# Filter rows moved behind a read-back, a stage placed three steps later, the last block split over four banks, and one product placed earlier

## The chip, the cores and the metric

The kernel runs on one core of one Trainium2 chip. The metric is the device time of one execution in microseconds (us). It is quoted as the median of several runs, with their range. The span of the profiled execution, which the profile measures, is some 2 to 3 us shorter than that time.

PE is TensorE's matmul, DVE is VectorE, ACT is ScalarE, POOL is GpSimd and SP is SyncE, which here only issues DMAs. An engine's name with a q behind it (SPq) is its sequencer, where DMA issues are recorded.

## The reference

```python
def _attn_ref(x, filt_r, filt_i):           # x: 8 x 3008 x 256
    X = np.fft.rfft(x, axis=1)
    F = (filt_r + 1j * filt_i)[None, :, :]
    return np.fft.irfft(X * F, n=x.shape[1], axis=1)

def _moe_ref(x, w_in, w_out, beta):         # 24064 tokens, 256 -> 2048 -> 256
    h = x @ w_in
    g = h * (1.0 / (1.0 + np.exp(-beta * h)))
    return g @ w_out
```

Each batch is filtered along its 3008 positions in the frequency domain. The result goes token by token through a feed-forward layer with a gated sigmoid.

## The kernel before

The feed-forward layer is the bulk: 47 blocks of 512 tokens, each in 16 steps, so 752 steps. A step has two large matmuls into `hps`, one ACT activation into `gT`, and four matmuls into `acc`. PE needs about 0.87 us for it, which is the distance from one activation to the next.

The filter is made of matmul stages. Batch 0 is filtered before the first step (the start). Batches 1 to 7 are filtered in pieces that a plan puts between the steps. For each of them the stages are: `s1` (first transform, written to a DRAM scratch d1), `a2_read` (d1 read back in another order), `s23` (second transform, spectrum times filter, first inverse transform), then a second trip through DRAM (d2), and `s4`. The "spectrum" below is `s23`; its first matmul needs the landed d1 read.

```python
# issue of the filter's rows, at the end of the start
for i in range(4):
    scale_wout(i)            # w_out was staged in frr's rows; POOL scales it out of there
for k0 in range(0, NK, JG):  # k0 = 0: SP issues; k0 = 8, 16, ...: POOL
    for at in (0, M):
        for go in load_filter(frr, filt_r, at, k0, JG, gp if k0 else nc.sync):
            go()             # 12 loads in all, 256 KB each
# ... cut ...
def s1(b, i, on_act):        # cut to the write
    ...
    if jj + 2 == JG:
        nc.sync.dma_start(s["d1r"][:, g * JG : (g + 1) * JG, :], s["a1"][:])

def a2_read(b):              # four reads, which wait until the writes have landed
    for h in range(NG):
        t = a2pool.tile([P, KG, D], BF16, name="a2", tag="a2")
        nc.sync.dma_start(t[:], s["d1c"][:, h * KG : (h + 1) * KG, :])
# ... cut ...
if B > 1:                    # batch 1's plan: place(first step, last step, pieces)
    at = place(1, 11, u1(1, True), per=2)
    place(at + 1, at + 1, [lambda: a2_read(1)], per=9)
    at = place(22, 54, u23(1), per=2)
    place(58, 58, [lambda: zz_read(1)], per=9)
    place(66, 78, u4(1), per=2)
# ... cut: the last block ...
acc = [opsum.tile([P, 2, D], F32, name="acc", tag="acc") for _ in range((nch + 1) // 2)]
...
    evac(ost[:, 2 * h : 2 * h + n, :], acc[h][:, :n, :], h == 0 and (i < 6 or last))
    if last:
        store(t0 + 2 * h * P, n * P, ost[:, 2 * h :, :], (nc.scalar, nc.sync)[h])
```

In the start, batch 0's first stage and the angle tables come interleaved:

```python
    for i in range(3, 5):
        first1(i, (False, False))
        warm(2)                      # matmuls on zeros, to keep PE occupied
    t2_more(0, nc.vector)            # three DVE copies within SBUF (lines 289 to 291)
    first1(5, (True, True))
```

## Time and profile before

| | before |
|---|---|
| median of 3 runs (range) | 794.76 us (793.23 to 795.56) |
| span of the profiled run | 791.4 us |
| start, up to batch 0's first `zz` transposes | 35.99 us |
| steps 0 to 100 (with the filter of batches 1 and 2) | 112.33 us |
| steps 100 to 751 | 633.40 us |
| tail, from the start of the last activation to the end | 6.03 us |

The four pieces, with 3.61 us between the transposes and step 0, make up the span. They are read from the start times of the 752 activations in the trace.

The page of the kernel before, cut to the busy times and the chain of work that ended last:

```profile
span 791.4 us, 15358 instructions
PE 776.2 (98%) x6097; PEld 547.4 (69%) x6097; DVE 393.2 (50%) x641; ACT 597.9 (76%) x920; POOL 149.3 (19%) x151
...
PE 88%; DMA 6%; DVE 3%; issue 1%; ACT 1%; SPq 0%; POOL 0%; DVEq 0%; POOLq 0%; ACTq 0%
```

Only 15 us of the span remain in which PE is not busy, and part of these is at the two ends. But 6% of the chain is DMA, so there are places where PE waits for a transfer. PE's waits, longest sum first (waiting tile and line, what it waited for: us in total, how many, the longest):

```profile
PE ps L621 <- DMA a<-d: 2.3, 2, 2.1
PE psa L347 <- DMA xg<-in_x_dram: 1.2, 1, 1.2
```

The first is the spectrum's first product in batches 1 and 2, waiting for the d1 read. The transfers behind the longer one are on SP's timeline (start, duration, sequencer, line, output from input, how many issues):

```profile
54.73 0.30 SPq L604 DMA_DIRECT2D d<-a  x1
62.77 1.78 SPq L611 DMA_DIRECT2D a<-d  x4
64.60 2.62 SPq L760 DMA_DIRECT2D out_dram<-ost  x4
```

and the product on PE's timeline, with its wait in brackets:

```profile
66.34 0.38 PE L621 MATMUL ps<-a,t 128*128 128x256 bf16 x2 [2.10 <-DMA a<-d]
```

The last d1 write is issued at 54.73 and the reads, which wait for its landing, go at 62.77. That is 8.0 us for a write of 384 KB. What else the DMA engines did is in the window view (busy time of each engine in the window; the last three columns are PE's granted clock, the DMA engines' busy share and what they moved in GB/s):

```profile
41.00:59.00 18.00, 17.91 (x143) 12.26 (x142) 7.19 (x11) 15.07 (x27) 8.21 (x10) 1.00 1.05 259
59.00:67.00 8.00, 5.90 (x51) 4.16 (x50) 2.08 (x4) 4.78 (x8) 0.00 (x0) 1.00 0.67 203
```

From 41 to 59 us the engines are full. POOL has issued eight filter loads of 256 KB there, among the d1 writes. The first and the last of the eight on POOL's timeline:

```profile
47.85 0.58 POOL L129 DMA_DIRECT2D frr<-in_filt_r_dram  x1
...
51.73 0.60 POOL L132 DMA_DIRECT2D frr<-in_filt_r_dram  x1
```

### The profile page before, as it was taken

The page shows a single profiled execution, that of the slowest core. Times are in us where ns is not written, and L with a number is a line of the kernel's source. Part 1 is how long each engine was busy: PE and PEld are TensorE (multiplying, and loading weights), DVE is VectorE, ACT ScalarE, POOL GpSimd, SP SyncE. Part 2 cuts the span into 40 slices and gives each one's busy share as a digit, 9 for nine tenths or more (in the row PEclk, how much of TensorE's full clock was granted, in tenths as well). Part 3 has the DMA queues.
Part 4 walks back from the last instruction along what each step waited for, and adds up shares of the span by engine and source line. Part 5 has one row for each costly group of instructions (what it writes and reads, how often), then busy time and mean ns, then how long its engine had stood idle before and what let it go on. Part 6 is the DMA issues. An engine that isn't in the chain of part 4 may idle for free.

```text
span 791.4 us, 15358 instructions
## 1 busy us (share of the span) xinstructions
PE 776.2 (98%) x6097; PEld 547.4 (69%) x6097; DVE 393.2 (50%) x641; ACT 597.9 (76%) x920; POOL 149.3 (19%) x151
## 2 busy tenths in 40 slices
PE   8898999999999999999999999999999999999997
PEld 5766667766777667876668766687667776776665
DVE  7846835755537464465534746267452761500000
ACT  6886886886678866788677876778767788677776
POOL 8542500330013200131002310024000340000000
PEclk9999999999999999999999999999999999999999
DMA  9994678116811178011960228412360214110101
GB/s 189 243 258 134 165 193 219 55 67 186 208 52 47 68 200 218 29 68 71 216 179 28 90 95 196 152 42 90 120 203 27 75 67 127 43 39 28 54 27 53
DMA packets 82579, 91.43 MB, mean 116 GB/s; under 512 B 3726, under 2 KB 72480, under 8 KB 81486
## 3 DMA queue, kind: packets, MB, share of 16 engines
q1 hardware_dynamic: 78460, 71.06, 28.9%
q0 software_dynamic: 3328, 18.35, 11.7%
q10 hardware_dynamic: 720, 1.05, 0.5%
q8 instruction: 47, 0.77, 0.4%
q14 instruction: 24, 0.20, 0.1%
HBM read 57.16 MB, written 46.66 MB: 131 GB/s over the span
## 4 chain that ended last, share of the span: by engine, by line
PE 88%; DMA 6%; DVE 3%; issue 1%; ACT 1%; SPq 0%; POOL 0%; DVEq 0%; POOLq 0%; ACTq 0%
PE acc L811 39%; PE hps L783 38%; PE ps L599 3%; DMA d<-a 2%; PE ps L522 2%; PE ps L621 2%; PE ps L647 2%; DMA fri<-in_filt_i_dram 1%; DVE ost L107 1%; DMA a<-d 1%; DMA xg<-in_x_dram 1%; DVE q_t L636 0%; ACT a L105 0%; DVE q_t L633 0%; DVE p_t L632 0%
## 5 line engine op out<-in xcount | busy, mean ns | idle before, releaser
L792 ACT ACTIVATE gT<-hps,beta_sb 128x512 bf16<-128x512 f32 x752 | 516.7, 687 | 177.6 <-PE hps L783 167.3
L811 PE MATMUL acc<-wout_sb,gT 128*128 128x256 bf16 x3008 | 454.9, 272 | 1.1 <-ACT ost L105 0.2
L783 PE MATMUL hps<-y,win_sb 128*128 128x512 bf16 (+7 forms) x1728 | 447.7, 351 | 0.3 <-DVE y L109 0.3
L811 PEld LDWEIGHTS <-gT 128*128 128x128 bf16 x3008 | 285.4, 98 | 132.3 <-issue 4.2
L783 PEld LDWEIGHTS <-win_sb 128*128 128x128 bf16 x1728 | 164.8, 98 | 24.8 <-issue 0.7
L637 POOL TENSOR_TENSOR v_t<-p_t,q_t 128x512 bf16<-128x512 f32 x84 | 106.8, 1271 | 370.2 <-DVE q_t L636 363.5
L107 DVE COPY ost<-acc 128x512 f32<-128x512 f32 x87 | 56.1, 683 | 195.3 <-PE acc L811 189.1
L107 DVE CAST a<-ps 96x512 bf16<-96x512 f32 x96 | 65.9, 686 | 86.6 <-PE ps L599 86.6
L109 DVE TENSOR_SCALAR y<-ps 128x376 bf16<-128x376 f32 (+2 forms) x120 | 64.5, 541 | 61.2 <-PE ps L522 61.0
L632 DVE TENSOR_TENSOR p_t<-ps,frr 128x512 f32<-128x512 f32 x84 | 58.1, 692 | 34.4 <-PE ps L621 29.3
L636 DVE TENSOR_TENSOR q_t<-ps,fri 64x512 f32<-64x512 f32 x84 | 58.3, 694 | 1.2
L633 DVE SCALAR_TENSOR_TENSOR q_t<-ps,fri 64x512 f32<-64x512 f32 x84 | 57.4, 684 | 1.1
L522 PEld LDWEIGHTS <-zz 96*128 96x128 bf16 x512 | 35.3, 97 | 29.6 <-DVE q_t L636 0.8
L105 ACT ACTIVATE z<-ps 128x512 bf16<-128x512 f32 x84 | 49.5, 590 | 0.4
L599 PE MATMUL ps<-xg,t 94*96 94x512 bf16 x112 | 41.9, 381 | 0.1
L522 PE MATMUL ps<-t,zz 96*128 96x94 bf16 x448 | 36.7, 204 | 0.0
L621 PE MATMUL ps<-a,t 128*128 128x256 bf16 x168 | 32.1, 273 | 2.3 <-DMA a<-d 2.3
L116 POOL DMA_DIRECT2D xg<-in_x_dram x22 | 12.3, 566 | 116.4 <-PE acc L811 97.7
L647 PE MATMUL ps<-v_t,t 128*128 128x256 bf16 x168 | 32.1, 273 | 0.3 <-DVE q_t L636 0.3
L621 PEld LDWEIGHTS <-t 128*128 128x128 bf16 x168 | 15.9, 98 | 17.1 <-issue 2.7
L599 PEld LDWEIGHTS <-t 94*96 94x96 bf16 x112 | 13.8, 123 | 11.9
L647 PEld LDWEIGHTS <-t 128*128 128x128 bf16 x168 | 15.4, 98 | 8.0 <-DVE q_t L636 0.5
(121 smaller groups left out, 198.7 us busy)
## 6 DMA issues: line engine op xcount, KB each, us to landing
out_dram<-ost SPq DMA_DIRECT2D x40, 512.0 KB, 2.8
d<-a SPq DMA_DIRECT2D x28, 384.0 KB, 6.4
a<-d SPq DMA_DIRECT2D x28, 384.0 KB, 4.8
d<-z SPq DMA_DIRECT2D x28, 384.0 KB, 2.6
zz<-d SPq DMA_DIRECT2D x28, 384.0 KB, 5.6
xg<-in_x_dram POOLq DMA_DIRECT2D x6, 1280.0 KB, 10.5
out_dram<-ost SPq DMA_DIRECT2D x20, 128.0 KB, 2.4
frr<-in_moe_w_out_dram POOLq DMA_DIRECT2D x4, 512.0 KB, 14.7
```

What stands on the lines that cost most here:

```text
L107: nc.vector.tensor_copy(dst, src)
L109: nc.vector.tensor_scalar_mul(dst, src, scale)
L522: nc.tensor.matmul(ps[:, e, :NP], lhsT=zz[:, jj + e, dc * P : (dc + 1) * P], rhs=tab[:], start=True, stop=True,)
L599: nc.tensor.matmul(ps[:KP], lhsT=t1[:], rhs=s["x"][:, 2 * i : 2 * i + 2, :], start=True, stop=True)
L621: nc.tensor.matmul(ps[:, e, :], lhsT=t2[:, k0 + e, 3:5, :].rearrange("p c k -> p (c k)"), rhs=s["a2"][g][:, kk + e, :], start=True, stop=True,
L632: nc.vector.tensor_tensor(p_t[:], ps[:], frr[:, ks_, :], ALU.mult)
L636: nc.vector.tensor_tensor(q_t[:M], ps[M:P], fri[M:P, ks_, :], ALU.mult)
L637: nc.gpsimd.tensor_tensor(v_t[:], p_t[:], q_t[:], ALU.add)
L647: nc.tensor.matmul(ps[:, e, :], lhsT=t3[:, k0 + e, :], rhs=v_t[:, e, :], start=True, stop=True)
L783: nc.tensor.matmul(hps[:, pos - t0 : pos - t0 + ln], lhsT=win_sb[:, dc, fb * P : (fb + 1) * P], rhs=ys[b][:, dc, n0 : n0 + ln], start=(dc ...
L792: nc.scalar.activation(gT[:, :tn], hps[:, :tn], ACT.Silu, scale=beta_sb[:, fb : fb + 1])
L811: nc.tensor.matmul(acc[tb // 2][:, tb % 2, :], lhsT=gT[:, tb * P : (tb + 1) * P], rhs=wout_sb[:, fb, :], start=(fb == 0 and tb % 2 == 0), ...
```

## The change

The intent: take the eight filter loads out of the d1 writes' way by queueing them on SP behind the d1 reads (rows 8 and up are needed only at the fifth spectrum product); give batch 1's spectrum three more steps; evict the last block in four halves with four stores; and move the first product of the start, and one eviction, where DVE should take them better. The diff, cut to its core:

```diff
@@ the start: first product moved up, one eviction from ACT to DVE
-    table3(0, 2, True)
-    table3(0, 0, False)
 ...
+    table3(0, 2, True)
+    product(0)
+    table3(0, 0, False)
     for i in range(NK // 2 + FLAG):
-        if i < NK // 2:
+        if 0 < i < NK // 2:
             product(i)
 ...
-            table3(1 + i // 3, 4 - 2 * (i % 3), i % 3 == 1 or i == 8)
+            table3(1 + i // 3, 4 - 2 * (i % 3), i % 3 == 1)
@@ the filter's rows
-    for k0 in range(0, NK, JG):
-        for at in (0, M):
-            for go in load_filter(frr, filt_r, at, k0, JG, gp if k0 else nc.sync):
-                go()
+    for at in (0, M):
+        for go in load_filter(frr, filt_r, at, 0, JG, nc.sync):
+            go()
 ...
+    def uf():                       # rows 8 and up
+        return [
+            go
+            for k0 in range(JG, NK, JG)
+            for at in (0, M)
+            for go in load_filter(frr, filt_r, at, k0, JG, nc.sync)
+        ]
@@ batch 1's plan
-        place(at + 1, at + 1, [lambda: a2_read(1)], per=9)
-        at = place(22, 54, u23(1), per=2)
-        place(58, 58, [lambda: zz_read(1)], per=9)
-        place(66, 78, u4(1), per=2)
+        place(at + 1, at + 1, [lambda: a2_read(1)] + uf(), per=9)
+        at = place(25, 56, u23(1), per=2)
+        place(60, 60, [lambda: zz_read(1)], per=9)
+        place(67, 79, u4(1), per=2)
@@ the last block: one bank, one eviction and one store for each 128 rows
+                    (fpsum if h % 2 else opsum).tile([P, 1, D], F32, name="acc", ...)
 ...
-                        store(t0 + 2 * h * P, n * P, ost[:, 2 * h :, :], (nc.scalar, nc.sync)[h])
+                        store(t0 + h * P, P, ost[:, h:, :], (nc.sync, nc.scalar)[h // 2])
```

## The prediction

> **What bounds it.** The page's busy line gives PE 776.2 of 791.4 us (98%) at full clock; the chain that ended last is 88% PE, 77 points of it the two large products (acc, hps). The Trainium skill ("Perfetto Trace Analysis", Identifying the Most-Contended Engine) warns that PE busy is no measure of the limit; here it only tells where PE idles. The change leaves the matrix work as it is, so it can win only idle time. PE's waits sum to about 9 us. The largest: 2.3 us in two waits of batch 1's and 2's first spectrum product (ps, L621) on the d1 read-back, the longer 2.1 us at 64.2 to 66.3. The rest are pieces of 0.2 to 1.2 us.
>
> **1. Filter rows behind the d1 reads.** In the window view the DMA engines are saturated (share 0.9 to 1.2) from 41 to 59 us. There POOL issues 8 frr loads of 256 KB (47.8 to 51.7) among the d1 writes. The last d1 write is issued at 54.7, lands 7.9 us later, and only at 62.8 can the reads go (3.5 us). "DMA: Bandwidth & Descriptors" (Issuing engines are not separate DMA queues) says that transfers of different issuers share the same 16 engines and interleave; the saturated share agrees. Without these loads I expect (estimate from about 230 GB/s here) the write to land at 57 to 60, the first read at 61 to 64.
>
> **2. Spectrum three steps later.** Step 25 begins near 67 us (three steps of 0.87 plus the work placed in them). Either move alone should remove the 2.1 us wait. The burst behind it (PE waiting 0.31 on DVE q_t at 74) should go too. Gain 2.1 to 2.5 us. Filter rows 8 and up are first needed at the fifth product, near 76 us; I expect them by 70 to 74.
>
> **3. Given back.** Batch 1's d2 read moves about 2 us later, into a stretch where DMA is saturated again (110 to 130). There batch 2's last d1 write takes 11.5 us, and its read reaches PE with no slack (0.17 us wait at 134.7). I expect that wait to become 0 to 2 us, about 0.7.
>
> **4. Start.** From 21.9 to 34.9 us DVE runs almost without gaps: it waited 0.86 us for fri rows, then works through products of 2 x 0.60. Moving the first product up 0.3 us only lengthens that wait. One t3b eviction goes from ACT (0.83) to DVE (a slot of 0.46), where it just fills the 0.46 us gap at 32. Net 0, within 0.3.
>
> **5. End.** Evictions of 0.60 (ACT) and 0.69 (DVE) and two stores of 256 KB become four half evictions (0.35 to 0.42, an estimate) and four stores of 128 KB (2.4 against 2.8 us to land). The last issue is no earlier, since two stores of 0.4 queue on each engine. Net -0.1, within 0.3.
>
> **Sum.** -2.3 + 0.7 + 0 - 0.1, and up to 0.4 more: about -2 us. 794.76 becomes **792.7 us**, 8 in 10 within **790.8 to 794.5**. Faster by over 2%: 0.01; within 2%: 0.98; slower: 0.01. Before's own runs spread by 2.3 us, so the sign is likely, not sure.
>
> **Signs.** Right if PE's L621 wait at 64 is gone, the last d1 write lands in under 5 us, no DVE p_t waits on frr, and the span is about 789.5. Step 3 shows in the L621 wait near 133. Step 4: zz's first transposes stay near 36.0.
>
> **Wrong if** the frr rows[...] come later than 76 us; if block 0's stores behind them hold the output tile; if the second d1 wait grows by more than 2 us; or if the start becomes DVE-bound.

## The result, and the profile after

| | before | after |
|---|---|---|
| median of 6 runs (range) | 794.45 us (793.23 to 795.56) | 791.66 us (789.83 to 793.29) |
| ratio, with its 95% interval | | 0.9965 (0.9944 to 0.9986) |
| span of the profiled run | 791.4 us | 790.8 us |
| start | 35.99 us | 38.38 us |
| steps 0 to 100 | 112.33 us | 110.18 us |
| steps 100 to 751 | 633.40 us | 633.42 us |
| tail | 6.03 us | 5.18 us |

A ratio here and below is the mean time of one kernel's runs over the mean of the other's runs of the same rounds, so it is not quite the ratio of the medians. The changed kernel is faster by 0.35%, which counts as the same within 2%. All outputs are right.

The table holds a puzzle. The middle won 2.15 us and the tail 0.85 us, but the profiled run's start was 2.39 us longer, so the span won only 0.6 us. The six times explain which is typical: 789.83, 789.99, 790.43 and 792.89, 793.05, 793.29. They are two groups, and the profiled run belongs to the slower one. The experiments have to say whether the start is a cost of the change.

The same lines of the page after:

```profile
span 790.8 us, 15274 instructions
PE 772.1 (98%) x6001; PEld 548.0 (69%) x6097; DVE 395.7 (50%) x643; ACT 596.9 (75%) x920; POOL 144.6 (18%) x143
...
PE 92%; DVE 3%; issue 2%; POOL 2%; ACT 1%; DVEq 0%; ACTq 0%; POOLq 0%
```

DMA has left the chain. The fall of PE's busy time from 776.2 to 772.1 is not saved work: weight loads still number 6097, while matmul records fell to 6001, because some are missing from this trace. PE's longest waits after:

```profile
PE psa L347 <- DMA xg<-in_x_dram: 2.8, 2, 2.3
PE pw L186 <- DVE wz L181: 1.2, 1, 1.2
PE pb L409 <- POOL tiny L308: 0.9, 1, 0.9
```

No wait on L621 is left, in batch 1 or 2. What leads now is the start: the waits for rows of x grew from 1.2 us (one) to 2.8 us (two, the longer one 2.28), and a wait of 0.9 us is new. The view puts that one down to POOL's `tiny`; but the product that waits, at 17.09 us, reads `a_t`, whose eviction DVE ended at 16.99. SP's timeline after:

```profile
57.11 0.30 SPq L604 DMA_DIRECT2D d<-a  x1
60.31 1.77 SPq L611 DMA_DIRECT2D a<-d  x4
62.18 0.37 SPq L129 DMA_DIRECT2D frr<-in_filt_r_dram  x1
```

The last d1 write now lands 3.2 us after its issue, not 8.0, and the filter loads follow the reads. The product starts without a bracket:

```profile
69.23 0.38 PE L621 MATMUL ps<-a,t 128*128 128x256 bf16 x2
```

The same windows as before:

```profile
41.00:59.00 18.00, 17.46 (x130) 11.59 (x131) 8.82 (x14) 15.35 (x29) 5.00 (x3) 1.00 0.70 185
59.00:67.00 8.00, 7.95 (x69) 5.80 (x68) 2.52 (x4) 6.18 (x11) 0.00 (x0) 1.00 0.79 251
```

The DMA share from 41 to 59 us fell from 1.05 to 0.70. PE is busy for 7.95 of the 8 us from 59 to 67, where it had 5.90. DVE's `p_t` products, which read the rows that come later now, show no wait for them.

**Batch 2's read.** The prediction feared a longer wait there. Before, from the chain that ended last (start, duration, what):

```profile
118.05 0.56 DVE y L109
118.61 0.12 SPq L760
...
119.89 11.48 DMA d<-a
...
131.38 3.28 DMA a<-d
...
134.71 0.38 PE ps L621 x2
```

After, SP's timeline and PE's:

```profile
119.86 0.57 SPq L604 DMA_DIRECT2D d<-a  x1
131.30 1.77 SPq L611 DMA_DIRECT2D a<-d  x4
```

```profile
134.94 0.38 PE L621 MATMUL ps<-a,t 128*128 128x256 bf16 x2
```

The write takes as long as before (11.4 us from its issue to the reads). But the steps are 0.6 us later on the clock in this run (step 80 starts at 132.21, before at 131.63) and the read is not, so it has slack and the wait of 0.17 us is gone.

**The tail.** Before, the last activation (ACT's timeline) and the last store (SP's):

```profile
785.33 0.69 ACT L792 ACTIVATE gT<-hps,beta_sb 128x512 bf16<-128x512 f32 x1 [0.18 <-PE hps L783]
...
787.44 0.37 SPq L746 DMA_DIRECT2D out_dram<-ost  x1
```

After (the last two stores are ACT's):

```profile
785.58 0.69 ACT L800 ACTIVATE gT<-hps,beta_sb 128x512 bf16<-128x512 f32 x1 [0.18 <-PE hps L791]
...
787.33 0.88 ACTq L754 DMA_DIRECT2D out_dram<-ost  x2
```

The last issue is not earlier: before it begins 2.11 us after the activation's start, after it begins about 2.19 us after it (half of the 0.88 for the first of two). The trace's packets show what is: the last store packet ends 4.35 us after the activation before, and 3.85 us after it in the changed kernel.

### The profile page after: what moved, and what is told of

It reads as the page before. It is cut to its first block, busy times and chain, and to the rows that moved or that the text cites. A ratio compares the mean times of both kernels' runs of the same rounds, so it can differ in the third digit from the quotient of the medians.

```text
span 790.8 us, 15274 instructions
## 1 busy us (share of the span) xinstructions
PE 772.1 (98%) x6001; PEld 548.0 (69%) x6097; DVE 395.7 (50%) x643; ACT 596.9 (75%) x920; POOL 144.6 (18%) x143
## 3 DMA queue, kind: packets, MB, share of 16 engines
q10 hardware_dynamic: 736, 1.05, 0.6%
## 4 chain that ended last, share of the span: by engine, by line
PE 92%; DVE 3%; issue 2%; POOL 2%; ACT 1%; DVEq 0%; ACTq 0%; POOLq 0%
PE acc L826 42%; PE hps L791 37%; PE ps L599 3%; PE ps L522 3%; PE ps L621 2%; PE ps L647 2%; DVE ost L107 1%; POOL xg L116 0%; POOL r L269 0%; DVE qb_t L442 0%; ACT a L105 0%; DVE pb_t L442 0%; PE pb L409 0%; PE psz L452 0%; DVE q_t L636 0%
## 5 line engine op out<-in xcount | busy, mean ns | idle before, releaser
L791 PE MATMUL hps<-y,win_sb 128*128 128x512 bf16 (+7 forms) x1634 | 427.4, 350 | 0.3 <-DVE y L109 0.3
L107 DVE COPY ost<-acc 128x512 f32<-128x512 f32 (+1 forms) x88 | 56.2, 677 | 193.6 <-PE acc L826 188.0
L522 PEld LDWEIGHTS <-zz 96*128 96x128 bf16 x512 | 35.3, 97 | 29.0
L621 PE MATMUL ps<-a,t 128*128 128x256 bf16 x168 | 32.1, 273 | 0.4
L621 PEld LDWEIGHTS <-t 128*128 128x128 bf16 x168 | 15.8, 98 | 14.6
```

The source lines that it names most:

```text
L107: nc.vector.tensor_copy(dst, src)
L522: nc.tensor.matmul(ps[:, e, :NP], lhsT=zz[:, jj + e, dc * P : (dc + 1) * P], rhs=tab[:], start=True, stop=True,)
L621: nc.tensor.matmul(ps[:, e, :], lhsT=t2[:, k0 + e, 3:5, :].rearrange("p c k -> p (c k)"), rhs=s["a2"][g][:, kk + e, :], start=True, stop=True,
L791: nc.tensor.matmul(hps[:, pos - t0 : pos - t0 + ln], lhsT=win_sb[:, dc, fb * P : (fb + 1) * P], rhs=ys[b][:, dc, n0 : n0 + ln], start=(dc ...
```

## The experiments

The theory at the start: the filter loads held up the d1 write; moving them or moving the spectrum would each remove the wait; the start's 2.4 us are an accident of this execution. The rivals: it is the shift that counts; the start's loss is caused by the moved product; the half clock that the profile shows in the changed kernel's start makes the slow group.

All times here are medians with their range, and ratios are against the kernel before in the same rounds. The runs of before had medians of 794.77, 793.91 and 794.99 us. "Start" and "middle" are as in the tables above: up to the `zz` transposes, and steps 0 to 100.

### e1_after_again, e2_filter_only, e3_shift_only, e4_end_only: the change again, and three parts of it alone

e1 is the changed kernel unedited. e2 has only the edit of the filter's rows (the SP loads behind batch 1's d1 reads, steps as before). e3 has only the new steps:

```diff
-        at = place(22, 54, u23(1), per=2)
-        place(58, 58, [lambda: zz_read(1)], per=9)
-        place(66, 78, u4(1), per=2)
+        at = place(25, 56, u23(1), per=2)
+        place(60, 60, [lambda: zz_read(1)], per=9)
+        place(67, 79, u4(1), per=2)
```

e4 has only the last block's edit.

> The changed kernel again, unaltered. In the first trace of it the time to batch 0's first transposes (pz) was 38.4 us against 36.0 before, with the granted clock at half from 11.6 to 15.0 us, and its six times lie in two groups near 790 and 793. My theory: this late start is a draw of the execution and no part of the change, so a run of the upper group shows the half clock between 8 and 16 us and pz near 38.4, a run of the lower group full clock and pz near 35.5 to 36; from pz on both take the same time (steps 0 to 100 in 110.2 us, tail 5.2 us). Rival: the late start belongs to the change, then every trace of the changed kernel has it and the groups come from somewhere else.

> Before, with the filter's later rows queued behind the d1 reads and nothing else. My theory: enough by itself, the last d1 write lands in under 5 us instead of 7.9, the 2.1 us wait of PE at the first spectrum product is gone, steps 0 to 100 take 110.0 to 110.6 us instead of 112.33. Rival: both moves are needed, then a wait of 0.5 us or more stays there. Start and tail as before (tail 6.0 us). About 2 us faster than before.

> Before, with batch 1's spectrum three steps later and nothing else; the filter loads stay on POOL. My theory: the read lands near 66.3 us as before, step 25 comes near 67, so the wait is gone here too, steps 0 to 100 in 110.0 to 110.6 us. Rival: the read is still short by part of the time, a wait of 0.5 us or more. About 2 us faster than before.

> Before, with the last block in four banks and four stores and nothing else. In the two traces the tail from the last sigmoid's start to the end fell from 6.03 to 5.18 us, where I had predicted 0.1. If that belongs to the four banks and stores: tail 5.1 to 5.3 us here, steps 0 to 100 at 112.3 as before. Rival: a chance of when the last store landed, then the tail lies anywhere from 5.2 to 6.1. About 0.8 us faster than before, near the noise.

| run | us (range) | ratio (95%) | d1 write issued, reads issued | wait of batch 1, of batch 2 | start | middle | tail |
|---|---|---|---|---|---|---|---|
| before's profile | | | 54.73, 62.77 | 2.10, 0.17 | 35.99 | 112.33 | 6.03 |
| e1 after again | 791.60 (789.71 to 793.55) | 0.9954 (0.9932 to 0.9977) | 56.82, 60.01 | 0, 0 | 38.33 | 109.95 | 5.18 |
| e2 filter only | 792.57 (791.27 to 793.52) | 0.9968 (0.9950 to 0.9986) | 56.56, 59.75 | 0, 0.35 | 38.07 | 110.13 | 5.75 |
| e3 shift only | 793.19 (791.35 to 794.05) | 0.9975 (0.9957 to 0.9993) | 54.66, 65.24 | 1.20, 0.26 | 36.07 | 112.59 | 6.03 |
| e4 end only | 794.65 (792.21 to 796.47) | 0.9993 (0.9970 to 1.0016) | 54.50, 64.87 | 3.68, 0 | 34.99 | 115.94 | 6.13 |

SP's timeline in e2, where the lines stand one lower:

```profile
56.56 0.30 SPq L603 DMA_DIRECT2D d<-a  x1
59.75 1.78 SPq L610 DMA_DIRECT2D a<-d  x4
```

and in e3:

```profile
54.66 0.30 SPq L604 DMA_DIRECT2D d<-a  x1
65.24 1.78 SPq L611 DMA_DIRECT2D a<-d  x4
```

What follows. The filter's move alone brings the landing from 8.0 to 3.2 us and removes batch 1's wait; its middle, 110.13 us, is the changed kernel's. The shift alone did not remove the wait in its trace: PE came to the product 3.2 us later than in before (67.42 against 64.24), but the reads went 2.5 us later too, the landing took 10.6 us, and the middle stayed at 112.59 us. The shift changes nothing before step 22, so this later landing is no effect of it. POOL's timeline of e3, the first and the last load, and PE's wait:

```profile
50.10 0.58 POOL L129 DMA_DIRECT2D frr<-in_filt_r_dram  x1
...
53.98 0.60 POOL L132 DMA_DIRECT2D frr<-in_filt_r_dram  x1
```

```profile
68.62 0.39 PE L621 MATMUL ps<-a,t 128*128 128x256 bf16 x2 [1.20 <-DMA a<-d]
```

POOL issued the loads 2.25 us later than in before, though the start and the d1 write came at the same times. In the four traces with the loads on POOL and the last d1 write at 54.5 to 54.7 us (before, e3, e4 and e5), the reads went 14.9 to 15.1 us after POOL's first load. So the loads, and not the start, set the landing there, and their time varies between executions: POOL first waits for `w_out` to land in the rows that they overwrite. With before's landing, which released PE at 66.34 us, the shift would have been enough in this trace. The six times of e3 fit that: their mean is 0.25% (2.0 us) below before's, and the interval, 0.07% to 0.43%, overlaps that of e2. The traced execution was the second slowest of the six. So the times do not show which of the two edits is worth more. The traces show that the filter's move takes away what delayed the landing, and that the shift did not cover the late landing of e3. What the shift did do is small: e2 still has a wait of 0.32 us on DVE's `q_t` at 74 us (before 0.31), which the changed kernel does not have there; but it has two such waits later, of 0.26 and 0.39 us, for 0.31 and 0.26 in before, so nothing was won there.

e4 is the surprise; neither its middle nor its tail came as expected. Up to the last block it has the same instructions as before, yet its middle took 3.6 us longer. Its start was 1.0 us earlier, at 34.99 us, and the wait grew to 3.68 us. PE's windows in e4 around the end of that wait (columns as above):

```profile
60.00:68.70 8.70, 5.02 (x40) 3.40 (x38) 1.97 (x4) 4.25 (x7) 0.00 (x0) 1.00 0.68 192
68.70:72.10 3.40, 3.40 (x17) 1.92 (x15) 2.49 (x4) 0.72 (x2) 1.26 (x1) 0.50 0.93 311
```

PE idled, and then its clock was halved for 3.4 us. The earlier start was lost twice. PE had waited 1.32 us for a DVE eviction of `a` at 53.1 us, so it came to the spectrum at 64.48 us, no earlier than in before. And POOL issued its loads at 49.94 us, 2.1 us later than in before, and the reads went 2.1 us later. So this execution does not show that the wait grows because the start is early; the later loads are enough for it. It did suggest that the start varies between executions of any version, and that the change decides whether a good start counts.

### e5_start_only, e6_after_warm, e7_before_warm, e8_after_old_end: the start, the half clock, and the end

In e1 and e2, as in the changed kernel's own profile, PE's clock was halved for 3.4 us in the start, after PE waited 2.3 to 2.4 us for x. The theory was that the half clock makes the slow group. e5 is before with only the start's edits (the first product moved up, one eviction to DVE). e6 is the changed kernel, and e7 the kernel before, with PE kept occupied over that wait by six more matmuls on zeros:

```diff
     for i in range(2):
         first1(i, (True, True))
-        warm(2)
+        warm(8 if i else 2)
```

e8 is the changed kernel with the last block as before.

> Before, with the first product moved up and the last t3b eviction on DVE, nothing else. My theory: no gain, from the fourth product's wait for the fri rows to pz 14.1 us as before (21.90 to 35.99) within 0.3; the start is early or late by the arrival of x and the granted clock alone. Rival: the late starts of the changed kernel come from this edit, then this run's times lie about 2 us above before, or in two groups 3 us apart. Steps 0 to 100 as before: 112.3 us, or up to 116 when the d1 wait is long enough that the clock falls, as in the end-only run.

> The changed kernel with six more warm-up matmuls (0.22 us each) in the place where PE waits for the third part of x. Theory: what splits the changed kernel's times into two groups is the half clock from 11.6 to 15 us that follows this wait. With the gap filled the clock stays full, pz comes by 36.7 even when x is late, and all six times lie between 789.5 and 791.3. Rival: the late x by itself makes the upper group, then pz is near 38 in a late run and the two groups stay.

> Before, with the same six warm-up matmuls. Theory: in the kernel before an early start is lost again, because the d1 read lands at a time set by the DMA queues (66 to 68.6 us) and PE waits for it; so the warm-up gains nothing here: median within 0.7 us of before, the d1 wait 2 us or more in the trace. Rival: start and d1 wait are independent, then this gains about as much as the warm-up gains on the changed kernel, 1 to 1.5 us.

> The changed kernel with the old last block: two banks, two stores of 256 KB. The end-only run had a tail of 6.13 us where the changed kernel has 5.18 twice; in it an instruction fetch of 8 KB fell among the last stores' packets. If four stores help unless a fetch falls there: tail 5.75 (as in the filter-only run, no fetch among them) to 6.03 here, steps 0 to 100 in 110.2, time 0.6 to 0.9 us above the changed kernel. Rival: the tail is set by the position of the instruction stream alone, then it can be 5.2 here too.

| run | us (range) | ratio (95%) | wait of batch 1, of batch 2 | start | middle | tail | half clock at |
|---|---|---|---|---|---|---|---|
| e5 start only | 794.54 (793.08 to 795.25) | 0.9999 (0.9983 to 1.0015) | 1.82, 0.25 | 36.03 | 111.86 | 6.04 | none |
| e6 after, warm | 790.54 (789.84 to 791.46) | 0.9953 (0.9938 to 0.9968) | 0, 0 | 36.14 | 109.93 | 5.19 | none |
| e7 before, warm | 797.12 (793.64 to 798.18) | 1.0025 (1.0004 to 1.0047) | 2.18, 1.79 | 37.35 | 115.64 | 6.03 | 137.7 |
| e8 after, old end | 790.58 (790.23 to 793.56) | 0.9960 (0.9942 to 0.9977) | 0, 0.10 | 35.11 | 111.07 | 5.74 | none |

What follows. The start's edits are worth nothing that shows: ratio 0.9999, and from the fourth product to the `zz` transposes 14.04 us in e5 against 14.09 in before. So the changed kernel's late start is not their doing; e2, e7 and e12, which lack these edits, started late too. The extra matmuls seemed to confirm the half clock: e6 was in one group, 789.84 to 791.46. e7 missed its expectation, a median within 0.7 us of before's: the same edit made the kernel before slower by 0.25%, with an interval just clear of none, and its trace has two waits and a half clock at the second. Its traced start was late, so the theory that an early start is lost again was not tested by it. The end is left to e12 below; e8 shows a tail of 5.74 with the old end, not 6.03. It was expected 0.6 to 0.9 us above the changed kernel and was not: an end worth about half a microsecond (see below) cannot be read from medians that move by more with the start. e8's middle is the only one with the filter's move above 110.2 us; PE waited 0.7 us for a DVE `a` eviction there.

### e9_warm_fri_sp, e10_warm_again, e11_after_third, e12_end_padded: the half clock on trial, a variant, and the tail

e10 is e6 again and e11 the changed kernel again, on the same chip, so that the half clock is judged in one set of rounds. e9 adds to e6 that the last rows of the other filter half are issued by SP behind their neighbours, not by ACT later:

```diff
-    for go in load_filter(fri, filt_r, 0, *FG[2], nc.sync):
-        go()
+    for f, at in ((filt_r, 0), (filt_i, M)):
+        for go in load_filter(fri, f, at, *FG[2], nc.sync):
+            go()
 ...
-    for go in load_filter(fri, filt_i, M, *FG[2], nc.scalar):
-        go()
```

e12 is about the tail. In 12 of the 14 traces an 8 KB instruction fetch (the profile's queue q14) fell among the last stores or after them; e2 and e8 have none behind the last activation. Before, e3, e5 and e7 have it in the tail, some 4.35 us after the last activation, and tails of 6.03 to 6.04 us. That is where their last store's packets end. In e4 it came at 3.25 us, among the four stores, and the tail was 6.13 us. The kernels with the filter's move have eight more issues on SP, and no fetch before the span has ended. So e12 is e4 with eight small stores added to SP's stream long before the end, and nothing else:

```diff
+    pad = dpool.tile([8, D], BF16, name="pad", tag="pad")
+    place(300, 300, [lambda i=i: nc.sync.dma_start(pad[i : i + 1, :], wout_sb[:1, 0, :])
+                     for i in range(8)], per=9)
```

> The changed kernel with the warm-up, and the last third of filt_i's rows in fri loaded from SP behind the others instead of from ACT. In the traces the fourth product waits for fri rows of the second third (pb at 21.9 us with full clock), which share the DMA engines with these early loads. If that contention sets it, the fourth product starts 0.5 to 1 us earlier, pz comes by 35.3 and the time falls 0.5 us below the warm-up alone. If the queue order on SP only moves the wait to the seventh product, no gain or a loss of up to 1 us.

> The warm-up version again, to be compared on one chip with the changed kernel: all six times in one group within 2 us near 790.5, half clock before 20 us absent. About 1 us under the changed kernel's median.

> The changed kernel a third time on the same chip as the warm-up version: two groups near 790 and 793 again; steps 0 to 100 in 109.9 to 110.3 us, no wait of PE over 0.3 us for the d1 read of batch 1 or 2, tail 5.18 us.

> The end-only version with eight extra stores of 512 bytes from SP at step 300, which do nothing but move SP's instruction stream to where the changed kernel has it. The end-only run's tail was 6.13 us with an instruction fetch of 8 KB among the last stores, the changed kernel's 5.18 without. If the stream's position decides: fetch gone from among the stores, tail 5.1 to 5.3. Rival: the tail differs for another reason (other engines' streams, buffers), then 6.1 again. The d1 waits of the kernel before stay: time 793.5 to 796.

| run | us (range) | ratio (95%) | wait of batch 1, of batch 2 | start | middle | tail | half clock at |
|---|---|---|---|---|---|---|---|
| e9 warm, rows by SP | 791.45 (790.77 to 793.35) | 0.9959 (0.9942 to 0.9976) | 0, 0 | 36.36 | 109.95 | 5.18 | none |
| e10 after, warm again | 791.94 (790.31 to 795.01) | 0.9962 (0.9941 to 0.9983) | 0, 0 | 38.85 | 110.05 | 5.18 | 16.7 |
| e11 after, third time | 792.57 (789.64 to 793.42) | 0.9960 (0.9941 to 0.9978) | 0, 0 | 35.33 | 109.97 | 5.18 | none |
| e12 end, padded | 793.21 (791.74 to 795.84) | 0.9980 (0.9960 to 1.0001) | 0.30, 0.30 | 38.96 | 110.40 | 5.18 | 16.5 |

What follows, first for the half clock: that theory fell. e10 had the extra matmuls and no half clock at the wait for x, and yet a start of 38.85 us (its clock was halved at 16.7 us, within a later wait of 2.44 us that ended at 17.09 us with `a_t`); its times were expected in one group and were not; and its times overlap those of e11. Moreover each run comes with its mean granted clock: of the ten runs in the changed kernel's slow group (the changed kernel, e1 and e11 together), three have 0.999 or 1.000, more than the 0.998 that one half clock of 3.4 us in 790 leaves. The other seven have 0.997 or 0.998, and the eight of the fast group 0.999 or 1.000. So the half clock often goes with a late start, but a late start does not need it. e9 did not beat the others, though the first half of its expectation held: its fourth product came at 20.84 us (before: 21.90), but then PE waited 0.8 us for ACT's `z_t`. No version is clearly faster than the changed kernel.

For the tail: e12 differs from e4 by eight instructions at step 300, and its tail is 5.18 us, not 6.13. The fetch moved from among the stores to 6.9 us, behind the end of the span. So the position of SP's stream decides; that it does so through the fetch fits all 14 traces and is inferred from them. With the fetch out of the way, two stores cost 5.74 to 5.75 us (e2, e8) and four cost 5.18 to 5.19 (the six traces of the changed kernel and its variants, and e12). With the fetch just behind them two cost 6.03 to 6.04, and with it among them four cost 6.13. So 0.29 of the change's 0.85 us goes with the fetch, which moved when the filter's loads moved to SP (e2 shows it alone), and 0.56 with the four stores, which need the fetch to be away.

For the start, the traces suggest another cause than the clock, and no experiment tests it. DVE's timeline in before:

```profile
12.80 0.35 DVE L289 TENSOR_SCALAR t<-t 128x768 bf16<-128x768 bf16 x1
13.06 0.35 DVE L290 COPY t<-t 128x768 bf16<-128x768 bf16 x1
13.33 0.35 DVE L291 COPY t<-t 128x768 bf16<-128x768 bf16 x1
```

and in the changed kernel's profiled run:

```profile
13.38 0.35 DVE L289 TENSOR_SCALAR t<-t 128x768 bf16<-128x768 bf16 x1
13.65 0.98 DVE L290 COPY t<-t 128x768 bf16<-128x768 bf16 x1
14.55 1.97 DVE L291 COPY t<-t 128x768 bf16<-128x768 bf16 x1
16.45 0.54 DVE L107 CAST a_t<-psa 128x384 bf16<-128x384 f32 x1
```

POOL's timeline of the same run:

```profile
11.61 2.81 POOL L269 TENSOR_SCALAR r<-u 128x768 f32<-128x768 f32 x1
14.50 1.81 POOL L270 TENSOR_TENSOR u<-u,r 128x768 f32<-128x768 f32 x1
```

Over all 14 traces, of these first three copies every one that started by 13.57 us took 0.35 us; those that started from 13.65 to 13.84 took 0.82 to 0.98; and those at 14.55 and 14.56 took 1.97 or 1.98, to just behind the end of POOL's operation at 16.31. (One at 14.28, between POOL's two operations, took 0.36.) The eviction of `a_t` behind them came later (16.45 against 13.88 us in these two traces), and so did the transposes of batch 0. The six traces with stretched copies are the six with long starts, 37.35 to 38.96 us; the other eight have 34.99 to 36.36. In the six, the third part of x to be used was first used at 10.14 to 10.43 us, in the eight at 9.34 to 9.66. The Trainium skill ("SBUF — State Buffer", SBUF: two separate sides) says that DVE and GpSimd share a pair of ports which is "an exclusive lock, not a bandwidth split", held for a whole instruction by the one that starts first while the other blocks. It says so for DVE operations in a two-port mode, or with two inputs in SBUF; whether these copies run in such a mode, no run here shows. The copy of 1.97 us beside POOL's 1.81 agrees with that. The copies of 0.35 us that ran within POOL's span of L269, 11.61 to 14.42, do not look like it, though POOL's spans are rough. A version with the copies placed earlier would test it; it was not run, so this stays an account that fits the traces, and why x arrives later in some executions stays open too.

**What the groups are.** The three runs of the changed kernel have 18 times: eight from 789.64 to 790.86 (mean 790.17) and ten from 792.48 to 793.55 (mean 792.95), with none between. The groups lie 2.8 us apart, and the traced starts of 35.33 and 38.33 to 38.38 us lie 3.0 us apart. The kernel before has no such gap in its 33 shared runs. In the six traces with the loads on POOL the middle varies instead, from 110.40 to 115.94 us, and it does not follow the start alone: 115.94 us for a start at 34.99 (e4), 112.33 and 112.59 for 35.99 and 36.07 (before, e3), 110.40 for 38.96 (e12, with a wait of only 0.30), but 115.64 for 37.35 (e7). The changed kernel's middle, with e6, e9 and e10, is 109.93 to 110.18 for starts from 35.33 to 38.85.

## Why the prediction was right or wrong

The predicted 792.7 us was 1.0 above the measured median of 791.66, and the range held. That it came so close is partly luck: three of the six runs fell in each group, and the median lies between them, where no run of the changed kernel was. Point by point:

1. **Filter rows behind the reads: right.** The write was to land at 57 to 60 and the read to go at 61 to 64. Measured in the changed kernel: issued at 57.11, landed by 60.31. e2 shows that this edit alone does it. The Trainium skill's statement that transfers of different issuers run on the same engines and interleave ("DMA: Bandwidth & Descriptors", Issuing engines are not separate DMA queues) agrees with this: with 16 engines at a share of 0.70 and not 1.05, the write took 3.2 us and not 8.0.
2. **"Either move alone should remove the 2.1 us wait": not so for the shift in its trace.** The step took the read's landing as fixed at 66.3 us and moved only PE's arrival. The landing is not fixed while the loads are among the writes; the reads went at 62.77 in before and at 65.24 in e3, behind POOL's later loads. e3 kept 1.20 us of wait and won nothing in its traced middle; its six times, 2.0 us faster on average, leave open that it won in others. The gain predicted for both together, 2.1 to 2.5 us, is what the profiled pair shows (2.15), so this error did not show in the sum. "The burst behind it should go too" failed: the 0.31 us went from that place and came back in others.
3. **Given back, +0.7 us: wrong in sign.** The longer wait in batch 2 did not come; it was 0 in six of the seven traces that have both moves and 0.10 in e8. The step took the d2 read's later place for a delay of the d1 write. The write still took 11.4 us, but it was issued earlier against the steps: its reads went 0.91 us before step 80 in the changed kernel, and 1.29 in e6 with an early start, against 0.25 in before. The traces tell what moved the issue. It comes 11.7 us before step 80 in the five traces with neither move, 11.9 with the shift alone (e3), 12.2 with the filter's move alone (e2), and 12.3 with both. So both moves contribute, the filter's more, and neither removed this wait alone (0.26 us in e3, 0.35 in e2). Why the filter's move acts here stays open.
4. **Start, net 0 within 0.3: right for the edit** (e5). But the prediction treated the start as a constant, and it varies by 3 us between executions of one program (35.33 to 38.38 in the changed kernel) and from 34.99 to 38.96 over all traces. The sign that it gave, transposes near 36.0, fails in six of the 14 traces, e2, e7 and e12 among them, which have no start edit.
5. **End, -0.1 us: right in direction, off in size.** The tail won 0.84 to 0.85 us in every trace with the whole change. The step argued from issue times, which did not improve indeed, and set the faster landing of the smaller stores against the queueing. Two terms were missed: four stores put the last packet down 0.5 us sooner (3.85 against 4.35 us), and an instruction fetch that sat behind the last stores left the tail.

With the measured terms the sum is -2.15 (batch 1 and 2) - 0.85 + 0 = -3.0 us, and the medians of the six runs differ by 2.8. This sum leaves out the starts, which differed by 2.39 us in the same two traces. The predicted -2.0 was short mainly by the 0.7 that was not given back and by the tail.

One thing the prediction did not see at all: in the kernel before, the wait can hide a late start. In e12 the start was 3.0 us later than in before and step 100 came only 1.0 us later; in e7 nothing was hidden. The change takes the wait away, so its gain is not one number. Between traces with early starts it is 3.85 us of span (791.35 in before, 787.50 in e11: start 0.66, middle 2.36, tail 0.85). Between the profiled pair, where the changed kernel started late, it is 0.6. These are single executions. The median of the changed kernel moves with the share of slow executions: 791.66 and 791.60 where three of six were slow, 792.57 where four were. That the slow ones are the ones with late starts is seen in three traced executions only (two slow with 38.3 us, one fast with 35.3).

## What to carry to other kernels

The wait for the transfer was set here by what else the DMA engines had to move; moving the consumer later helps only if the landing stays where it was, so first look at what runs among the writes, and at more than one execution. When a wait in the middle absorbs some of the variation ahead of it, removing it makes the earlier stage's good and bad executions visible: look at single times for groups before explaining one profile's start. And check the last microseconds of a kernel for fetches of instructions: a change far away that adds a few instructions (eight here) can move a fetch in or out of the tail.

## What the Trainium skill lacked or had wrong

- "TensorE: Matmul & The Clock Gate" (Part 1: The HAM clock gate) has the half clock come after at least one idle window of about 3.4 us. Each fall here before the tail did last 3413 ns at 0.50, as the page's window has it, but it came with shorter waits of PE: at the end of one of 1.79 us (e7), some 1.4 us behind one of 2.28 (after), and within waits of 2.44 and 2.48 (e10, e12); one of 3.68 us (e4) had one behind it too. Waits of 2.10 us (before) and 2.18 (e7's first) had no fall behind them, so the length of one wait does not decide it.
- "SBUF — State Buffer" (SBUF: two separate sides) has DVE and GpSimd exclude each other for a whole instruction when DVE is in a two-port mode or has two inputs in SBUF. The copy stretched from 0.35 to 1.97 us agrees; three copies of 0.35 us within the recorded 2.81 us of a POOL instruction (before, 12.80 to 13.68 us) do not show it, with the reserve that POOL's spans are rough and that the copies' mode is not shown.
- "DMA: Bandwidth & Descriptors" (Queues, rings and completion order) lists the runtime's own row 14 without a cost, and no page was found with a figure for an instruction fetch beside a kernel's last stores. Here one 8 KB fetch on the profile's q14, behind or among them, went with tails longer by 0.29 us (two stores) and 0.95 us (four stores).
- No page that was used here says that the start of one and the same program varies by some microseconds between executions; here it was 35.33 and 38.38 us in two traces of the changed kernel, and 36.14 and 38.85 in two of the warm-up version.
